# q and k of the first twelve tiles in 2-KB rows on one queue, their bias from 64-row matmuls, and a new order

## Chip, cores and metric

The kernel runs on one core of a Trainium2 chip. The metric is the time of one execution on the device, in microseconds (us). Five engines work side by side, each through its own list of instructions in order: TensorE (PE, with its weight loads as PEld), VectorE (DVE), ScalarE (ACT), GpSimd (POOL) and SyncE (SP), which here issues nearly all DMAs.

## What is computed

Attention with a window of 96 keys, 8 global keys and a linear bias by distance, for 4 batches of 8 heads, 768 positions and 64 columns; its output, as 3072 rows of 512, goes through three products whose maximum is taken, and a last product.

```python
B, H, S, D = q.shape                                    # 4, 8, 768, 64
scores = scale * np.matmul(q, k.transpose(0, 1, 3, 2))
is_global = pos[None, :] < 8
is_local = (rel >= 0) & (rel < 96)
dist = np.where(is_global & ~is_local, 96.0, np.abs(rel))
scores = scores - slopes[:, None, None] * dist
scores = np.where(is_global | is_local, scores, -1e9)
a = softmax(scores)
x = np.matmul(a, v).transpose(0, 2, 1, 3).reshape(B * S, H * D)
h = np.maximum(np.maximum(x @ w1, x @ w2), x @ w3)      # 512 -> 768
out = h @ w_out                                         # 768 -> 512
```

## The kernel before, in words

The 3072 rows are 24 tiles of 128. A batch has six tiles; two neighbouring tiles make a part n (0 to 11), which is what one load of q (s = 0), k (s = 1) or v brings. The tiles are grouped into seven chunks of 4, 2, 2, 4, 4, 4 and 4 tiles for the expert products.

All work is cut into units, and a text, SCHEDULE, lists the units in the order in which their instructions go to the engines. A unit is a letter, its indices and, last, a number that says how it is done (0 for ACT, 1 for DVE, 2 for POOL in most of them). No scheduler moves anything afterwards: each engine runs its own share of the list in order and waits for what it needs.

- `l`, `v`, `w`, `o` load a part of q or k (line 156), a part of v, expert weights (line 478) and output weights. A part of q or k is read either in 512-byte rows (two positions of a head) or in 2-KB rows (eight positions); `short_rows` (line 149) decides: parts 6 to 11, and k of parts 0 to 2, have 512-byte rows. All loads are on SP's queue, but k of part 0, which is on ACT's.
- `c` casts a part of q or k to bf16 (line 179), `C` a half of v (line 190), `W` and `Q` weights. `x` (line 243) transposes a cast part on PE into PSUM and copies it to qkT, or, with 9, by a DMA.
- `Y` and `V` copy pieces of v, `G` (line 229) the global keys, `Z` (line 207) the first tile's keys into a tile of their own, kf.
- `S` (line 293) computes the scores of tile T for half of the heads (g): for each, matmuls of 64 rows (the 64 columns of a head) and 128 columns, two heads at a time in the two halves of the array, then the exponential on ACT (line 317) into P. In the first tiles (last index 1) the bias is added in PSUM ahead of the scores, by two matmuls of the identity with bias (line 299); later tiles multiply P by wmask, the exponential of the bias, on DVE (`M`, line 329). `K` (line 324) makes wmask of a head on ACT, `B` (line 319) the bias.
- `A` (line 338) multiplies P by v and normalises on DVE; `T` (line 376) transposes the result to xT, on PE with a copy (0, 1, 6, 8) or by a DMA (4).
- `F` c.f.j (line 417) is the product of chunk c with the columns f of expert j: four matmuls into one of three PSUM buffers (h), then a cast on ACT for j = 0, a maximum on DVE for j = 1 and 2. `O` (line 451) is the output product of a tile and its store, `E` the last tiles.
- `D` puts matmuls of zeros on PE at the start.

The lines that a sentence cannot say are those of the scores and of the bias:

```python
296         if how:
298             for hh in range(2):
299                 nc.tensor.matmul(sp[:, hh, :, 0:n], identb, bias[:, g, hh, :, sets(T)],
300                                  start=True, stop=False, skip_group_check=True)
301         for ds in range(n):
302             for i in range(2):
303                 jp = 2 * g + i
304                 for z in range(2):
305                     hsl = slice(64 * z, 64 * z + 64)
306                     nc.tensor.matmul(sp[:, z, i, ds], k_cols(T, hsl, jp, ds), q_cols(T, hsl, jp),
```

Of the kernel before, what the change touches and what calls it, by code (L numbers as in the profile page):

```python
# [12 lines left out]
FP32 = mybir.dt.float32  # L13
# [12 lines left out]
    K7 l1.0 c1.0.2 K6 l1.1 B6.1 D0.4 D4.4 B5.1 D2.0 D5.4 K0 c0.1.1 c0.0.1 K2 D8.0 B0.1 B4.0 B1.0  # L26
    B3.0 x0.1.3 K1 K3 K5 c1.1.2 B7.0 x0.0.7 D1.1 D9.2 S1.0.1 Z0.1 B2.1 v0 C0.0.2 S1.1.1 G1.0 x1.0.8
    K4 M1.0 S0.0.1 M0.0 v1 x1.1.8 S2.1.1 S2.0.1 M2.0 C0.1.2 Y0.1.2 Y1.0.1 M1.1 V2.1 Y0.0.1 G2.1 A1.2
    S0.1.1 C1.0.2 C1.1.2 Y2.0.0 Y1.1.2 D3.1 S3.0.1 M3.0 M0.1 A0.2 S3.1.1 M3.1 l2.0 c2.0.2 x2.0.6
    T1.1 M2.1 A2.0 V3.2 T0.0 G3.0 A3.1 l2.1 c2.1.2 x2.1.6 T2.1 w0.0 W0.0.0 l3.0 w0.1 S4.0.1 M4.0  # L30
    T3.8 V4.2 W0.1.2 S4.1.0 D7.1 G4.0 w0.2 F0.1.0 F0.0.0 S5.1.0 c3.0.1 x3.0.6 M4.1 w1.0 W1.0.0
    S5.0.0 F0.1.1 W0.2.2 F0.1.2 v2 C2.0.0 C2.1.0 W2.0.1 F0.0.1 F0.0.2 M5.0 F0.3.0 F0.2.0 M5.1 Y2.1.1
    V5.1 F0.5.0 w1.1 W1.1.0 W2.1.1 F0.4.0 A4.1 A5.0 F0.5.1 T4.0 F0.4.1 w1.2 W1.2.0 l3.1 T5.1 F0.2.1
    F0.2.2 l4.0 c4.0.1 W2.2.0 F0.5.2 c3.1.0 x3.1.7 Z1.0 F0.4.2 F1.0.0 F1.2.0 l4.1 c4.1.1 S7.0.0
    S6.1.0 l5.0 x4.0.6 l5.1 o0 F1.0.1 F1.0.2 c5.0.1 M7.0 F1.3.0 F1.4.0 F1.4.1 o2 c5.1.1 x4.1.7
    S6.0.0 S7.1.0 G7.0 v3 F1.2.1 F1.2.2 F1.3.1 Q2.1 F0.3.1 M7.1 Q0.0 F1.5.0 F1.5.1 S8.0.0 x5.0.7
    S8.1.0 G8.1 C3.0.2 C3.1.1 Y4.0.1 F0.3.2 F1.5.2 A7.0 F1.4.2 F1.1.0 M6.0 x5.1.6 v5 o1 Q1.0 v4
    S9.0.0 S9.1.0 l7.0 l6.1 C5.0.1 C5.1.0 F1.1.1 F1.3.2 Y3.1.1 M8.0 F1.1.2 T7.0 v6 l6.0 M6.1 v7
    Y3.0.1 M9.0 O0.2.1 l7.1 C4.0.0 O0.0.0 G9.0 V8.1 A6.1 c7.0.1 M8.1 c6.1.1 x6.1.9 O0.3.0 C4.1.0
    Y4.1.1 O0.1.1 Y5.1.0 S10.1.0 T6.8 V9.1 M9.1 S10.0.0 O1.0.0 A8.1 M10.1 T8.4 F2.0.0 x7.0.9 G10.0  # L40
    F2.4.0 c6.0.0 l8.1 v9 l9.1 F2.0.1 F2.1.0 M10.0 F2.0.2 S11.0.0 c7.1.0 Y5.0.1 x6.0.6 S11.1.0 V10.1
    F2.1.1 M11.0 F2.4.1 C6.0.0 A9.0 F2.2.0 V11.1 l9.0 O1.1.1 S13.1.0 x7.1.6 S13.0.0 G13.0 M11.1
    F2.2.1 F2.1.2 C6.1.1 F2.2.2 A11.1 F2.3.0 F2.5.0 A10.0 Y6.1.0 Z2.0 F2.4.2 T11.0 F2.5.1 F2.3.1
    C7.0.0 S12.1.0 T9.8 S12.0.0 F2.3.2 v8 C7.1.1 F2.5.2 M12.0 S14.1.0 T10.6 S14.0.0 c8.1.0 O2.0.0
    l8.0 M13.0 G14.1 Y7.1.1 M12.1 F3.2.0 V15.0 M13.1 c9.1.1 x9.1.9 F3.0.0 Y7.0.1 A13.1 F3.3.0 l11.1
    T13.4 M14.0 x8.1.9 M14.1 F3.0.1 S15.1.0 Y6.0.0 S15.0.0 F3.3.1 F3.3.2 F3.1.0 M15.0 M15.1 V14.0
    F3.4.0 c8.0.1 c9.0.0 x9.0.9 l10.0 F3.0.2 A12.1 F3.2.1 x8.0.9 C9.0.0 C8.0.0 A14.0 F3.1.1 T12.4
    l10.1 G15.1 Y8.0.1 c11.1.0 O2.1.0 A15.1 F3.5.0 F3.1.2 C9.1.1 F3.2.2 T15.8 S19.0.0 M19.0 S19.1.0
    c10.0.0 T14.4 C8.1.0 Y8.1.0 F3.4.1 l11.0 v10 F3.5.1 F3.5.2 F3.4.2 Y10.0.1 M19.1 Z3.1 S16.0.0
    S16.1.0 G16.1 V20.0 O3.3.0 O3.2.1 A19.1 F4.5.0 c10.1.1 x10.1.9 v11 F4.1.0 V16.1 G19.1 x10.0.9  # L50
    Y9.0.1 S18.1.0 S17.0.0 M17.0 M16.1 F4.3.0 F4.3.1 F4.5.1 M16.0 V17.1 F4.1.1 S17.1.0 S18.0.0
    F4.2.0 Y9.1.0 O3.0.0 M18.0 M17.1 C10.0.1 M18.1 A16.1 F4.1.2 T19.4 O3.1.1 A18.0 A17.1 C11.0.1
    c11.0.0 x11.0.9 F4.0.0 F4.2.1 F4.2.2 F4.3.2 T18.4 S20.1.0 S20.0.0 T16.4 T17.4 x11.1.9 C10.1.1
    Y10.1.1 F4.0.1 G20.1 F4.0.2 F4.5.2 S21.0.0 S21.1.0 G21.0 M20.0 F4.4.0 F4.4.1 C11.1.1 F4.4.2
    M21.1 F5.1.0 F5.2.0 V21.1 O4.2.1 F5.3.0 Y11.1.0 F5.3.1 M20.1 S22.0.0 S22.1.0 F5.2.1 F5.5.0
    Y11.0.0 F5.2.2 V23.1 F5.4.0 A20.1 F5.3.2 M22.0 M21.0 G22.0 S23.0.0 M23.0 S23.1.0 T20.4 F5.5.1
    O4.1.1 A21.1 T21.4 M23.1 M22.1 O4.0.0 V22.0 F5.4.1 F5.0.0 A23.1 T23.4 O4.3.0 A22.0 F5.4.2 F5.5.2
    F5.0.1 F5.1.1 F5.0.2 T22.4 F5.1.2 F6.3.0 F6.5.0 F6.4.0 F6.5.1 F6.4.1 F6.4.2 O5.1.0 F6.3.1 F6.1.0
    O5.3.1 F6.1.1 F6.0.0 F6.0.1 F6.0.2 O5.0.1 F6.2.0 F6.2.1 F6.3.2 O5.2.0 F6.2.2 F6.1.2 F6.5.2 E
    D6.0  # L60
"""


@with_exitstack
def kernel(
# [13 lines left out]
    nc = tc.nc  # L79
# [13 lines left out]
    sizes = [4, 2, 2, 4, 4, 4, 4]  # L93
# [36 lines left out]
    bias = persist.tile([128, 2, 2, 2, 3, 128], BF16, name="bias")  # L130
    vo_first = [persist.tile([128, 2 * H * 65], BF16, name=f"vof{i}") for i in range(2)]
    vo_next = [persist.tile([128, 2 * H * 65], BF16, name=f"vo{i}") for i in range(2)]
    ve = [persist.tile([128, 2 * H * 65], BF16, name=f"ve{i}") for i in range(2)]
    vf = [persist.tile([128, H * 65], BF16, name=f"vf{i}") for i in range(2)]
# [440 lines left out]
```

## Time and profile before

| what | value |
| --- | --- |
| time, median of 3 runs | 176.9 us (176.84 to 177.01) |
| profiled execution: its span, first to last instruction | 174.9 us |
| median less that span | 2.0 us |
| first expert matmul (h) starts | 21.8 us |
| last matmul ends | 171.5 us |
| PE busy | 169.3 us, 97% |
| DVE, ACT, POOL busy | 132.5, 120.1, 14.3 us |
| read from and written to memory | 25.17 and 6.29 MB |

The profile is of one execution, whose time is told by its span; the runs' times also hold what lies around the span, here 2.0 us. In the rows of the timeline the columns are the start, the length in us (of a group, from its first start to its last end), the engine, the line, the operation, the tiles written and read, their shapes and the count; in brackets stands the idle time ahead of it and what ended it. In a row of the chain they are start, length, engine, tile and line. In a row of groups, the total, the mean of one in ns, and the idle time ahead.

### The profile page before, as it was taken

To read this page: it belongs to the slowest core of one execution; us is meant where nothing else is said; L and a number is where in the kernel's file an instruction comes from. 1 tells how busy PE (TensorE), PEld (TensorE's weight loads), DVE (VectorE), ACT (ScalarE), POOL (GpSimd) and SP (SyncE) were. 2 spreads that over 40 slices of the span, in tenths; PEclk is the share of its full clock that TensorE was granted. 3 is DMA by queue.
4 is the path that set the end of the run, shared out by engine and by line. 5 is a ranking of instruction groups with operands and counts; after the bars stand their busy time and mean duration, and the time that the engine had idled before them with its cause. 6 is when DMAs were issued, how large, how long until landed. Compare 5 with 4: busy or idle time off the path is not lost.

```text
span 174.9 us, 4233 instructions
## 1 busy us (share of the span) xinstructions
PE 169.3 (97%) x1683; PEld 93.0 (53%) x1683; DVE 132.5 (76%) x288; ACT 120.1 (69%) x188; POOL 14.3 (8%) x25
## 2 busy tenths in 40 slices
PE   6999999999999999999999999999999999999992
PEld 2445654658684587754545545544455544444451
DVE  6668859889999999998978769995569873444510
ACT  6989999789988999999948977345594413121132
POOL 5269250000100000000000000000000000000000
PEclk9999999999999999999999999999999999999999
DMA  4999999999999999976999997563101750031205
GB/s 137 347 302 335 359 350 383 385 380 312 309 282 265 298 289 228 292 213 193 257 195 185 304 233 172 166 133 60 54 10 30 105 171 0 0 119 36 89 27 213
DMA packets 55507, 35.92 MB, mean 205 GB/s; under 512 B 18368, under 2 KB 47936, under 8 KB 55488
## 3 DMA queue, kind: packets, MB, share of 16 engines
q1 hardware_dynamic: 54304, 35.07, 73.9%
q10 hardware_dynamic: 1184, 0.59, 1.3%
q8 instruction: 13, 0.21, 0.5%
q14 instruction: 6, 0.05, 0.1%
HBM read 25.17 MB, written 6.29 MB: 180 GB/s over the span
## 4 chain that ended last, share of the span: by engine, by line
PE 94%; ACT 2%; DVE 1%; issue 1%; ACTq 0%; DVEq 0%
PE h L424 53%; PE po L439 18%; PE sp L306 7%; PE op L360 6%; PE wp L504 4%; PE tpr L261 2%; PE sp L299 2%; PE xtp L411 1%; ACT qkT L268 1%; ACT wo L496 1%; PE oph L360 1%; ACT P L317 1%; PE xtr L401 0%; PE tpp L282 0%; DVE qkT L285 0%
## 5 line engine op out<-in xcount | busy, mean ns | idle before, releaser
L424 PE MATMUL h<-xT,w 128*128 128x512 bf16 (+1 forms) x504 | 100.8, 349 | 0.0
L424 PEld LDWEIGHTS <-w 128*128 128x128 bf16 x504 | 46.7, 98 | 40.7 <-ACT w L493 0.6
L317 ACT ACTIVATE P<-sp 128x1024 bf16<-128x1024 f32 (+1 forms) x48 | 44.0, 956 | 9.2 <-PE sp L306 9.1
L429 ACT CAST h<-h 128x512 bf16<-128x512 f32 (+1 forms) x42 | 21.9, 531 | 22.1 <-PE h L424 22.1
L439 PE MATMUL po<-wo,ht 128*128 128x512 bf16 (+2 forms) x156 | 34.1, 363 | 0.0
L431 DVE TENSOR_TENSOR h<-h,h 128x512 bf16<-128x512 bf16 (+1 forms) x42 | 25.2, 605 | 10.9 <-PE h L424 8.9
L433 DVE TENSOR_TENSOR ht<-h,h 128x512 bf16<-128x512 bf16 (+1 forms) x42 | 25.5, 609 | 6.3 <-PE h L424 5.0
L334 DVE TENSOR_TENSOR P<-P,wmask 128x1024 bf16<-128x1024 bf16 x33 | 22.0, 684 | 2.0 <-ACT P L317 1.9
L439 PEld LDWEIGHTS <-ht 128*128 128x128 bf16 x156 | 14.3, 98 | 15.1 <-DVE ht L433 0.2
L448 ACT COPY ost<-po 128x512 f32<-128x512 f32 (+2 forms) x16 | 8.8, 553 | 15.8 <-PE po L439 15.3
L373 DVE TENSOR_TENSOR xb<-op,rz 128x512 bf16<-128x512 f32 x22 | 15.2, 692 | 0.8
L360 PEld LDWEIGHTS <-P 128*128 128x128 bf16 x352 | 13.4, 97 | 4.4 <-issue 0.7
L306 PE MATMUL sp<-qkT 64*128 64x128 bf16 x320 | 14.3, 218 | 0.1
L306 PEld LDWEIGHTS <-qkT 64*128 64x128 bf16 x320 | 9.3, 94 | 8.2 <-issue 5.1
L448 DVE COPY ost<-po 128x512 f32<-128x512 f32 (+1 forms) x10 | 6.5, 647 | 8.4 <-PE po L439 8.4
L188 DVE CAST qkp<-rawp 128x1024 bf16<-128x1024 f32 x12 | 8.2, 687 | 1.7 <-DMA rawp<-in_k_dram 1.6
L504 PE MATMUL wp<-zeros 128*128 128x512 bf16 x17 | 7.1, 559 | 1.5 <-DVE zeros L518 1.4
L188 ACT CAST qkp<-rawp 128x1024 bf16<-128x1024 f32 x8 | 8.4, 1050 | 0.0
L268 ACT COPY qkT<-tpr 128x512 bf16<-128x512 bf16 x12 | 6.6, 588 | 1.0 <-PE tpr L261 1.0
L268 DVE COPY qkT<-tpr 128x512 bf16<-128x512 bf16 x6 | 4.0, 688 | 3.9 <-PE tpr L261 3.9
L372 DVE RECIPROCAL rz<-op 128x8 f32<-128x8 f32 x22 | 4.4, 199 | 2.5 <-PE op L360 2.3
L360 PE MATMUL op<-vo,P 128*128 128x65 bf16 x128 | 5.4, 193 | 0.3 <-issue 0.3
(84 smaller groups left out, 127.9 us busy)
## 6 DMA issues: line engine op xcount, KB each, us to landing
rawv<-in_v_dram SPq DMA_DIRECT2D x12, 512.0 KB, 7.0
out_dram<-ost SPq DMA_DIRECT2D x23, 256.0 KB, 2.4
rawp<-in_k_dram SPq DMA_DIRECT2D x8, 512.0 KB, 5.9
rawp<-in_q_dram SPq DMA_DIRECT2D x12, 256.0 KB, 5.8
wst<-in_moe_w_dram SPq DMA_DIRECT2D x3, 1024.0 KB, 11.5
rawp<-in_q_dram SPq DMA_DIRECT2D x6, 512.0 KB, 6.2
wst<-in_moe_w_dram SPq DMA_DIRECT2D x3, 512.0 KB, 8.5
rawp<-in_k_dram SPq DMA_DIRECT2D x6, 256.0 KB, 8.6
```

What stands on the lines that cost most here:

```text
L188: copies[how](qk, src)
L306: nc.tensor.matmul(sp[:, z, i, ds], k_cols(T, hsl, jp, ds), q_cols(T, hsl, jp), start=not how, stop=True, skip_group_check=True)
L317: nc.scalar.activation(dst, src, AF.Exp, bias=0.0, scale=scale)
L334: nc.vector.tensor_mul(P, P, wmask[:, g, :, 0:2])
L360: nc.tensor.matmul(o, P[:, i, ds], vs[ds][:, h], start=(ds == 0), stop=(ds == len(vs) - 1), skip_group_check=True)
L373: nc.vector.tensor_tensor(out=x.rearrange("p (g h) d -> p g h d", g=2), in0=o4[:, :, :, 0:64], in1=rz[:, :, :, None].to_broadcast([128, 2, ...
L424: nc.tensor.matmul(ps, w123[f // 2][:, dm, j, (f % 2) * 128:(f % 2) * 128 + 128], xT[c][:, dm], start=(dm == order[0]), stop=(dm == order[ ...
L429: nc.scalar.copy(h01, ps)
L431: nc.vector.tensor_max(h01s[c, f], h01s[c, f], ps)
L433: nc.vector.tensor_max(ht[c][:, f], h01s[c, f], ps)
L439: nc.tensor.matmul(po, ht[c][:, f, tt * 128:(tt + 1) * 128], wo[:, f, cols], start=(f == 0), stop=(f == NF - 1))
L448: copy(ost, po)
```

## The change

- Parts 0 to 5 of q and k are all read in 2-KB rows: `SHORT` is empty, so k of parts 0 to 2 changes. All of them are on SP's queue. For k this also changes the pattern of the copy after the transposes (the one of 2-KB rows in place of that of 512-byte rows).
- The bias of the first tiles is built by matmuls of 64 rows. Their weights are the identity scaled by a head's slope (`slope_id`, made by `B`, 192 columns so that both halves can be cut from it), their moving side the distances in bf16 (`rbqb`, and `rbqs` with its halves of rows exchanged). For each half of the heads there are eight such matmuls of 256 columns in place of two of 128 rows and 512 columns. To fit this, the pairs of heads are dealt to g in another way (`jp = 2 * i + g`).
- kf and the unit `Z` are gone: a batch's first tile takes its keys from qkT by matmuls of 64 rows and 64 columns, eight in place of four.
- The tiles of v are views of one tile, vall, whose columns of ones one memset fills instead of eight.
- The identity is made first on POOL, the distances behind it.
- `U` is `S` for both halves. The tiles with a biased half 0 were 0 to 4 and 0 to 3 for half 1; now tiles 0 to 3 have both.
- New ways: casts split between two engines (`c` with 3 to 5), copies of v by a DMA (`Y` with 3).
- SCHEDULE is another list. By its units, x of 20 tiles is transposed by a DMA (`T` with 4) where 12 were; POOL takes 14 casts of q and k for 4, 12 of v for 5, 4 of weights for 2, and 21 copies of v's pieces for 4; the matmuls of zeros are 14 for 17.

The core of the diff, with the list itself left out:

```diff
     def short_rows(n, s):
-        return n >= 6 or (s == 1 and n < 3)
+        return n >= 6 or (n, s) in SHORT
...
-            dma = nc.scalar if (n, s) == (0, 1) else nc.sync
-            dma.dma_start(out=r, in_=src.rearrange("h (i e) d -> i h (e d)", e=2))
+            queues[how].dma_start(out=r, in_=src.rearrange("h (i e) d -> i h (e d)", e=2))
...
-                nc.sync.dma_start(out=r[:, z], in_=src[4 * z:4 * z + 4].rearrange("h (i e) d -> i h (e d)", e=ET))
+                queues[(how + z * (how == 2)) % 2].dma_start(out=r[:, z], in_=src[4 * z:4 * z + 4].rearrange("h (i e) d -> i h (e d)", e=ET))
...
         if how:
-            for hh in range(2):
-                nc.tensor.matmul(sp[:, hh, :, 0:n], identb, bias[:, g, hh, :, sets(T)],
-                                 start=True, stop=False, skip_group_check=True)
+            for i in range(2):
+                for part in range(2):
+                    for z in range(2):
+                        rows = slice(64 * z, 64 * z + 64)
+                        nc.tensor.matmul(sp[:, z, i, 0:n], slope_id[rows, 4 * z + 2 * i + g, 64 * part:64 * part + 128],
+                                         (rbqb, rbqs)[part][rows, sets(T)],
+                                         start=(i == 0 and part == 0), stop=False, skip_group_check=True)
         for ds in range(n):
             for i in range(2):
-                jp = 2 * g + i
+                jp = 2 * i + g
                 for z in range(2):
                     hsl = slice(64 * z, 64 * z + 64)
+                    if T % NT == 0:
+                        for e in range(2):
+                            nc.tensor.matmul(sp[64 * e:64 * e + 64, z, i, 0], qkT[T // NT][hsl, 1, e, jp, 0:64],
+                                             q_cols(T, hsl, jp), start=not how, stop=True, skip_group_check=True)
+                        continue
...
     def u_B(h, how):
-        mul(bias[:, g, z, i], rbq, -slopes[h] / scale)
+        mul(slope_id[:, h], ident, -slopes[h] / scale)
...
-    K7 l1.0 c1.0.2 K6 l1.1 B6.1 D0.4 D4.4 B5.1 D2.0 D5.4 K0 c0.1.1 c0.0.1 K2 D8.0 B0.1 B4.0 B1.0
+    B7.0 l0.0.0 D0.4 D5.6 K2 B2.1 B3.1 c0.0.3 l0.1.0 c0.1.1 x0.0.6 B0.2 B4.2 B6.0 B1.0 D6.2 B5.1
```

What the list changes is seen on the engines. ACT's rows from its start to the first cast of an expert product (h), before. Here wmask is the exponential of the bias, P that of the scores, tpr and xtp are transposes in PSUM, wst a raw weight:

```order
L326 ACTIVATE wmask<-rbq 128x384 x4
L322 ACTIVATE bias<-rbq 128x384 x3
L326 ACTIVATE wmask<-rbq 128x384 x3
L322 ACTIVATE bias<-rbq 128x384
L268 COPY qkT<-tpr 128x8x64 x2
L317 ACTIVATE P<-sp 128x1024 x2
L233 COPY qkT<-qkT 128x8x4
L326 ACTIVATE wmask<-rbq 128x384
L317 ACTIVATE P<-sp 128x4x128
L317 ACTIVATE P<-sp 128x1024 x2
```

ACT's rows now, from the first P to the last wmask (slope_id is the scaled identity; the three wmask and three slope_id ahead of the first P are not shown):

```order
L333 ACTIVATE P<-sp 128x1024 x4
L241 COPY qkT<-qkT 128x8x4
L276 COPY qkT<-tpr 128x8x64 x2
L333 ACTIVATE P<-sp 128x1024
L431 COPY xT<-xtp 128x4x128
L333 ACTIVATE P<-sp 128x1024 x2
L448 CAST h_680<-h 128x512
L333 ACTIVATE P<-sp 128x1024
L276 COPY qkT<-tpr 128x8x64
L448 CAST h_718<-h 128x512
L345 ACTIVATE wmask<-rbqb 128x384 x2
L333 ACTIVATE P<-sp 128x1024 x2
```

Five of the eight wmask rows have moved from ACT's start to behind the first casts of h (three more follow the last row shown), and the weight cast that stood ahead of the first h is no longer on ACT. Ahead of the four P shown first stand two P, a cast of v, two P of a first tile and half a cast of q.

DVE's rows in the first chunk's expert products, from the first maximum, before (P<-P,wmask is a mask, h<-h,h and ht<-h,h are the maxima of an expert product):

```order
L334 TENSOR_TENSOR P<-P,wmask 128x1024
L431 TENSOR_TENSOR h_605<-h_605,h 128x512
L433 TENSOR_TENSOR ht<-h_605,h 128x512
L493 CAST w_2_119<-wst 128x4x256
L431 TENSOR_TENSOR h_612<-h_612,h 128x512
L433 TENSOR_TENSOR ht<-h_612,h 128x512
L334 TENSOR_TENSOR P<-P,wmask 128x1024 x2
```

The same place now:

```order
L450 TENSOR_TENSOR h_718<-h_718,h 128x512
L450 TENSOR_TENSOR h_680<-h_680,h 128x512
L512 CAST w_2_112<-wst 128x4x256
L452 TENSOR_TENSOR ht<-h_718,h 128x512
L452 TENSOR_TENSOR ht<-h_680,h 128x512
L353 TENSOR_TENSOR P<-P,wmask 128x1024 x2
L512 CAST w_1_111<-wst 128x4x256
L353 TENSOR_TENSOR P<-P,wmask 128x1024 x4
L450 TENSOR_TENSOR h_817<-h_817,h 128x512
```

Six masks and a weight cast now stand in one run ahead of the next maximum; before, masks stood between maxima in ones and twos. POOL, which before had two weight casts left at this time and then almost nothing, now runs this:

```order
L199 CAST qkp<-rawp 128x1024
L512 CAST w_0_110<-wst 128x4x256
L208 COPY vall<-vall 64x520
L208 COPY vall<-vall 4x520
L512 CAST w_1_111<-wst 128x4x256
L202 CAST vall<-rawv 128x8x64
L208 COPY vall<-vall 64x520
L208 COPY vall<-vall 4x520
L512 CAST w_1_111<-wst 128x4x256
L199 CAST qkp<-rawp 128x1024
```

These are weight casts, casts of q and v, and copies of v's pieces that ACT and DVE did before.

More of the change, by code (lines that the diff above doesn't have):

```diff
@@ L187, in cast_part @@
         qb["p", n, s] = qk
+        if how >= 3:
+            for z, copy in zip(range(2), split[how - 3]):
+                if short_rows(n, s):
+                    copy(qk[:, z], src[:, z])
+                else:
+                    copy(qk[:, :, z], src[:, :, z])
+            return
         copies[how](qk, src)
@@ L518 @@
         nc.vector.memset(zeros, 0.0)
-        near, own = rbq[:, 0:2].rearrange("p s (e i) -> p s e i", e=2), rbq[:, 2]
+        make_identity(nc, identb)
+        nc.vector.tensor_copy(ident[:, 128:192], ident[:, 0:64])
+        nc.gpsimd.iota(dist, base=128, pattern=[[-1, 2], [1, 2], [2, 64]], channel_multiplier=-2,
+                       allow_small_or_imprecise_dtypes=True)
+        near, own = rbqb[:, 0:2].rearrange("p s (e i) -> p s e i", e=2), rbqb[:, 2]
         nc.gpsimd.affine_select(out=near, in_=dist, compare_op=ALU.is_ge, fill=BIGD, base=128,
@@ L523 @@
                                 pattern=[[1, 2], [-1, 2], [-2, 64]], channel_multiplier=2)
[L524 removed]
+        nc.gpsimd.memset(rbqb[0:NG // 2, 0:2], float(NL))
+        gap = rtmp[:, 0]
+        nc.vector.tensor_scalar(out=gap, in0=dist[:, 0].rearrange("p e i -> p (e i)"), scalar1=shift, scalar2=None, op0=ALU.add)
         nc.vector.memset(far, BIGD)
```

134 lines of the change are left out of this document (65 added, 69 removed).

## The prediction

> **What bounds the kernel now.** I read the page first, then the busy time by stretches, then the chain and the timelines of the start. TensorE (PE) is busy for 97% of the span and makes 94% of the chain that ends last.
>
> ```profile
> span 174.9 us, 4233 instructions
> ...
> PE 169.3 (97%) x1683; PEld 93.0 (53%) x1683; DVE 132.5 (76%) x288; ACT 120.1 (69%) x188; POOL 14.3 (8%) x25
> ...
> PE 94%; ACT 2%; DVE 1%; issue 1%; ACTq 0%; DVEq 0%
> ```
>
> A busy PE may still be a waiting PE, so I split the span where the first expert matmul (h) starts, at 21.8 us, and ask for busy time and for PE's waits in each part.
>
> ```profile
> 8.30:21.80 13.50, 12.84 (x234) 7.53 (x234) 10.81 (x29) 12.33 (x20) 8.53 (x12) 1.00 1.14 330
> 21.80:171.50 149.70, 149.64 (x1412) 82.53 (x1411) 116.53 (x236) 100.86 (x156) 3.02 (x3) 1.00 0.73 193
> ```
>
> The columns after the length are PE, weight loads, VectorE (DVE), ScalarE (ACT), GpSimd (POOL), the granted clock, the DMA share and GB/s. From 21.8 us on PE is busy for 149.64 of 149.70 us, at full clock, and the list of its waits is empty for that stretch. The groups of the chain there have the length of their columns:
>
> ```profile
> 24.48 7.01 PE h L424 x32
> ...
> 34.42 0.22 PE xtp L411 x4
> ...
> 72.95 0.11 PE sp L306 x4
> ...
> 91.85 0.22 PE xtr L401 x8
> ```
>
> 32 h matmuls in 7.01 us are 0.876 us for each product of four, waiting included. So the stage after 21.8 us is bound by PE's own work, and only work taken off PE, or new waits, can change it. Ahead of 21.8 us it is another engine:
>
> ```profile
> 3.11 2.10 ACT L326 ACTIVATE wmask<-rbq 128x384 bf16<-128x384 f32 x4 [0.43 <-DVE rbq L530]
> 5.12 1.33 ACT L322 ACTIVATE bias<-rbq 128x384 bf16<-128x384 f32 x3
> ...
> 8.27 1.04 ACT L268 COPY qkT<-tpr 128x512 bf16<-128x512 bf16 x2
> 9.80 1.94 ACT L317 ACTIVATE P<-sp 128x1024 bf16<-128x1024 f32 x2 [0.49 <-PE sp L306]
> 11.62 0.22 ACT L233 COPY qkT<-qkT 128x32 bf16<-128x32 bf16 x1
> ...
> 12.24 0.60 ACT L317 ACTIVATE P<-sp 128x512 bf16<-128x512 f32 x1
> ...
> 18.86 0.58 ACT L412 COPY xT<-xtp 128x512 bf16<-128x512 bf16 x1
> ...
> 20.54 1.05 ACT L493 CAST w<-wst 128x1024 bf16<-128x1024 f32 x1
> ...
> 23.41 1.09 ACT L429 CAST h<-h 128x512 bf16<-128x512 f32 x2
> ```
>
> From the first exponential (P) at 9.80 to the cast of the first weights, which ends at 21.59, ACT hardly rests (12.33 of the 13.5 us above). The first h follows that cast. After the last matmul, from 171.5 to 174.9, come a copy and a store, 3.4 us, which the change does not touch.
>
> **The first expert matmul.** To cost it I need the rows of DVE and PE at the start too:
>
> ```profile
> 7.45 0.41 PE L261 MATMUL tpr<-identb,qkp 64*128 64x64 bf16 x16
> ...
> 10.90 1.29 DVE L268 COPY qkT<-tpr 128x512 bf16<-128x512 bf16 x2 [1.61 <-PE tpr L261]
> ...
> 14.74 0.16 DVE L364 RECIPROCAL rz<-oph 128x4 f32<-128x4 f32 x1
> ...
> 14.94 0.42 DVE L365 TENSOR_TENSOR xb<-oph,rz 128x256 bf16<-128x256 f32 x1
> ...
> 18.40 0.20 DVE L372 RECIPROCAL rz<-op 128x8 f32<-128x8 f32 x1
> 18.63 0.69 DVE L373 TENSOR_TENSOR xb<-op,rz 128x512 bf16<-128x512 f32 x1
> ...
> 20.91 0.41 DVE L412 COPY xT<-xtp 128x512 bf16<-128x512 bf16 x1
> 21.27 0.49 DVE L404 COPY xT<-xtr 128x256 bf16<-128x256 bf16 x2
> ```
>
> Step one is when the first P can start. The landings are read from the engines that waited for them:
>
> ```profile
> 5.56 0.69 DVE L188 CAST qkp<-rawp 128x1024 bf16<-128x1024 f32 x1 [1.59 <-DMA rawp<-in_k_dram]
> ...
> 6.41 0.69 DVE L188 CAST qkp<-rawp 128x1024 bf16<-128x1024 f32 x1 [0.16 <-DMA rawp<-in_q_dram]
> ...
> 7.40:11.40 4.00, 3.84 (x63) 1.98 (x62) 2.19 (x4) 3.51 (x7) 2.11 (x3) 1.00 1.21 292
> 30.00:38.00 8.00, 8.00 (x86) 4.40 (x85) 7.29 (x15) 6.23 (x9) 0.00 (x0) 1.00 1.05 384
> ```
>
> The stretch from 7.4 to 11.4 us carries rows of 512 bytes, at 292 GB/s; the one from 30 to 38 carries rows of 2 KB, at 384 GB/s. A load of 524 KB takes 1.80 us at the one rate and 1.37 at the other, so each of the three k loads that change their rows saves 0.43 us. Before, k and q of tiles 0 and 1 are there at 6.41; with both in 2-KB rows I put it at 6.0. One queue instead of two may cost start-up: from nothing up to 1 us. From there, by rows: cast 0.69, sixteen transposes 0.41, two DVE copies of 0.65 (the long rows need the pattern of line 268, in place of a faster one), scores 0.4 and 0.1 of handing over; that is 8.9 us for the first P, 0.9 earlier than now.
>
> Step two is ACT's list from there to the copy of tile 2's transposed x, in the new order (the second piece of order above, and what the sentence behind it names): two P 1.94, a v cast and half a q cast of 0.6 each (as the half P), two half P 1.2, four P 3.9, a small copy 0.22, two transposed copies 1.04, one P 0.97, the copy 0.58. These are 11.1 us, and about 0.5 for two places where the list waits for its own last result (the scores of tile 2 behind DVE's copies, those of tile 4 behind ACT's). That gives 20.5. DVE has its own list. After the first scores it copies the transposed k and q of the second load, 2 x 1.29, done at 12.4. Then, to the copy that ends tile 3: three pairs of half normalisations (4 x 0.58 + 1.2 = 3.5), half a cast and a v cast 0.8, two copies 1.29, two small ones 0.4, one normalisation 0.89, and xT copies of 0.41, 0.49 and 0.41: 8.2 to 8.5 us, so 20.9. The first weights are the tenth load, 6.0 + 5 x 1.37 + 3 x 1.80 = 18.3 at the latest; POOL's cast of them (1.2, shown below) ends by 19.5 and does not gate. So **the first h starts at 20.9** instead of 21.81. Of the seven wmask exponentials and four bias scalings that ACT does ahead of the first P now (0.53 and 0.44 each), three and three remain, the latter on half the columns.
>
> The bias matmuls cost the same if the 64-row ones run in pairs: eight of 256 columns in pairs are four times 107 ns, as two of 512 columns are now. The row that bears on it is the scores' own, eight 64-row matmuls of 128 columns in pairs; the group of four above takes 0.11 us, half of what four in sequence need at 53 ns. Bounds: nothing to 0.43 us more per unit, eight units. They lie beside P (0.97 each), so I take nothing.
>
> **After the first h.** Before, 149.7 us of PE work follow. Eight transposes of x go from PE to the DMA queue (tiles 4, 5, 6, 7, 9, 10, 11, 15), at the 0.22 of the rows above: 1.8 us less. Scores of tile 5 (0.22) and x of the fourth k load (0.23) now stand ahead of the first h: 0.45 less. The first tiles of three batches use eight matmuls of 64 rows by 64 columns in place of four: between 0.11 us (four at a time) and 0.22 (pairs) per unit, six units, 0 to 0.7 more; I take 0.3. That leaves 147.8 us.
>
> The Trainium skill's page "TensorEngine Tiling (Array Packing)", Key Properties, says that different tiles of the array can run weight loads and matmuls in parallel, and lists four tiles for 64x64. The trace agrees for two (0.11 us for four); no run here shows four. By the page my 0.3 would be 0, and the last matmul at 169.4.
>
> ```profile
> xT<-xb SPq DMA_TRANSPOSE x12, 2.5
> ...
> 38.40:80.00 41.60, 41.55 (x573) 28.74 (x573) 40.00 (x95) 39.13 (x68) 0.62 (x1) 1.00 1.05 276
> ```
>
> Then comes a new wait. Five wmask exponentials now stand between ACT's h casts. By the rows ACT runs from 20.5: two P, an h cast (0.55) to 23.0; P, copy, h cast to 25.0; two exponentials, two P, three exponentials to 29.6; then the casts of the h of columns 4, 5, 2, 3 are done at 30.1, 30.9, 32.5 (a weight cast of 1.05 stands between) and 33.0. PE reaches the tenth product after nine (7.9), scores and transposes (1.1), at 29.9; h has three PSUM buffers, so this one needs column 4's, free at 30.1, and the twelfth, at 31.9, needs column 2's, free at 32.5. That is 0.2 + 0.6, and I add 0.2 for the DMA transpose of tile 5, which lands about when the next chunk begins (2.5 us to land). **1.0 us**, with bounds of 0 and 4.
>
> Weights: w2's first piece is the twelfth load instead of the eleventh, 1.37 later, less 3 times 0.43: it lands when it does now. The copies that go from ACT and DVE to POOL, the k copies for first tiles that vanish, the one memset in place of eight: none is on PE's path after 21.8 us. DVE is busy for 40.0 of the 41.6 us from 38.4 to 80, ACT for 39.1, and still PE waits for neither; both get less to do. I cost them at nothing, and the first rival says what it is if that cover goes.
>
> The sum, in the profiled execution: 20.9 + 147.8 + 1.0 = 169.7 us for the last matmul, where it is 171.5 now. That is 1.8 us less: a span of 173.1 instead of 174.9. The median of the runs, 176.9, lies 2.0 above the span; with that unchanged, **175.1 us**.
>
> **The rivals.**
>
> *DVE and POOL block each other: slower.* POOL goes from 14 us of work to about 40.
>
> ```profile
> 13.21 1.59 POOL L191 CAST vo<-rawv 128x512 bf16<-128x512 f32 x2 [0.20 <-DMA rawv<-in_v_dram]
> ...
> 14.23 0.59 DVE L233 COPY qkT<-qkT 128x32 bf16<-128x32 bf16 x1
> ...
> 21.68 0.68 DVE L188 CAST qkp<-rawp 128x1024 bf16<-128x1024 f32 x1
> 21.89 2.53 POOL L493 CAST w<-wst 128x1024 bf16<-128x1024 f32 x2 [3.20 <-DMA wst<-in_moe_w_dram]
> L233 DVE COPY qkT<-qkT x7: 155/171/594, 14.2 to 117.3; 128x32 bf16<-128x32 bf16 x7
> L493 POOL CAST w<-wst x2: 1040/1200/1359, 21.9 to 23.4; 128x1024 bf16<-128x1024 f32 x2
> L334 DVE TENSOR_TENSOR P<-P,wmask 128x1024 bf16<-128x1024 bf16 x33 | 22.0, 684 | 2.0 <-ACT P L317 1.9
> ```
>
> A DVE copy whose median is 171 ns took 594 and ended with POOL's cast, at 14.8; a POOL cast that began under a DVE cast took 1359 ns, the next one 1040. So each holds the other off. In the new order DVE has seven operations in a row, six masks of 0.68 and a weight cast, before the maxima that free h's buffers; POOL has some 5 us of copies and casts for the same time. One by one, they would put DVE back by up to 4.5 us, and PE with it, three buffers later. Taken at 3.8: 178.9. It decides from 1.8 us on. Against it: DVE's copies out of PSUM beside POOL were not longer, and half of DVE's work after 21.8 us reads PSUM. The Trainium skill's page "SBUF — State Buffer", Who interferes with whom, speaks against this change: a DVE instruction with two SBUF inputs contends with a GpSimd one that reads SBUF, and the second fully blocks. The two rows agree for copies and casts; no row shows it for the masks. By that rule 178.9 is nearer than the forecast.
>
> *The list on ACT is shorter than I think: faster still.* If the first loads land a whole us earlier on the one queue, ACT's list starts at 8.0, and the exponentials fall into holes: 20.0 + 147.5 + 0 = 167.5, 4.0 less, 172.9. For it: ACT was full from 9.8 on, so every us there counts. Against: v's landing also holds the list.
>
> *The 64-row bias does not run in pairs: no change.* Then a unit is 0.86 + 0.22 on PE, over P's 0.97; with the changes of tile shape 0.2 to 0.3 more per unit, about 0.9 in all to the first h, and a stall of 2 instead of 1: 21.8 + 147.8 + 2 = 171.6, or 177.0.
>
> **How the numbers follow.** Forecast 0.42, its own range 173.6 to 176.5; faster still 0.20; blocking 0.24; no change 0.14. About 0.2% is what a measurement of this kernel can tell from none, 176.55 to 177.25. Faster takes the first two and a little of the last: 0.63; within 0.2%: 0.11; slower 0.26. The range leaves out a fifth, a part of the fastest case (0.08) and half of the slowest (0.12): 172.4 to 178.9.
>
> **What would show it.** In the new profile: first P near 8.9, first h near 20.9, the last matmul near 169.7; PE waits of some 1 us between 29 and 34 us for ACT's h casts, and none after; DVE's masks between 27 and 34 us at 0.68 each (beyond 0.9 the blocking is right); the first tiles' score group of eight at 0.11 to 0.22 us. I am wrong if the first h starts after 21.8, if the list of PE's waits after 40 us is not empty, or if DVE's maxima rather than ACT's casts hold the buffers.

## The result and the profile after

The changed kernel takes **188.45 us** (median of 4 runs, 187.2 to 189.64), the kernel before 176.87 beside it: a ratio of 1.066, 95% interval 1.061 to 1.070. The forecast of 175.1 is 13 us too low, and the range ended at 178.9. All times below are medians; the kernel before stood at 176.76 to 176.88 beside each of the runs. Some executions of a kernel come out over 1.5% above its fastest, and these are left out of the medians of the experiments.

The page of the changed kernel (busy times, the DMA share by slices of 4.7 us, the DMA queue, the chain that ends last):

```profile
span 186.6 us, 4323 instructions
...
PE 167.9 (90%) x1689; PEld 93.9 (50%) x1710; DVE 128.9 (69%) x263; ACT 102.9 (55%) x165; POOL 45.1 (24%) x64
...
DMA  5899999938999999789998899877202333101116
...
q1 hardware_dynamic: 57520, 36.78, 75.6%
...
PE 49%; DMA 28%; DVE 7%; SPq 5%; ACT 3%; POOL 3%; issue 2%; ACTq 0%; POOLq 0%; DVEq 0%
PE h L443 31%; DMA rawv<-in_v_dram 12%; PE po L458 12%; DMA rawp<-in_k_dram 10%; DMA qkT<-qkp 5%; PE op L379 3%; SPq L171 3%; PE sp L322 2%; DVE h L450 2%; DMA xT<-xb 2%; DVE P L353 2%; ACT P L333 1%; SPq L167 1%; POOL qkp L199 1%; DVE xb L392 1%
```

The chain was 94% PE before. Now 28% of it are DMAs: loads of v and k, and transposes. The other engines are *less* busy than before, all but POOL. From the first expert matmul to 0.2 us before the last matmul ends, at 183.4 (the stretch for which the prediction had 148.8 us):

```profile
23.10:183.20 160.10, 149.40 (x1343) 81.99 (x1364) 111.92 (x214) 85.97 (x138) 30.59 (x38) 0.99 0.75 185
```

PE is busy for 149.40 of 160.10 us, so it stands for 10.7 us, where it stood for 0.06 before. The list of PE's waits (total, times, longest) names 9.3 of them; the rest are gaps of 0.05 to 0.3 us, in part where a matmul's record is missing. Its rows, the largest first:

```profile
PE h L443 <- ACT h L448: 3.1, 1, 3.1
...
PE sp L322 <- DMA qkT<-qkp: 1.5, 2, 1.3
PE h L443 <- DMA xT<-xb: 1.5, 2, 1.2
...
PE oph L379 <- DVE h L450: 1.3, 1, 1.3
```

The chain shows what stands behind them (start, length, what):

```profile
41.60 3.04 DMA rawp<-in_k_dram
...
45.43 8.62 DMA rawv<-in_v_dram
...
79.18 7.12 DMA rawv<-in_v_dram
...
86.90 0.59 ACT h L448
...
87.53 0.59 PE h L443
...
104.66 7.26 DMA rawp<-in_k_dram
...
113.11 4.35 DMA qkT<-qkp
...
126.70 3.48 DMA xT<-xb
```

One of them followed through: v of part 8 is issued at 79.18 and lands at 86.30, since other transfers stand ahead of it. ACT's list has its cast ahead of an h cast; the h cast at 86.90 gives back the buffer for which PE waits 3.1 us, until 87.53. The row of PE's wait names ACT; the cause is a load.

The queue's own time is its share of the span. Before it was

```profile
q1 hardware_dynamic: 54304, 35.07, 73.9%
```

or 129.3 us of 174.9 on 16 engines; now it is 75.6% of 186.6, or 141.1. The packets of the queue took 12 us more, most of it in those of 256 bytes: the eight added transposes bring 4096 more of them, and all of them together took 34.3 us, 23.9 before.

### The profile page after: what moved, and what is told of

Its sections match the earlier page's. It is cut to its first block, busy times and chain, and to the rows that moved or that the text cites. A ratio compares the mean times of both kernels' runs of the same rounds, so it can differ in the third digit from the quotient of the medians.

```text
span 186.6 us, 4323 instructions
## 1 busy us (share of the span) xinstructions
PE 167.9 (90%) x1689; PEld 93.9 (50%) x1710; DVE 128.9 (69%) x263; ACT 102.9 (55%) x165; POOL 45.1 (24%) x64
## 3 DMA queue, kind: packets, MB, share of 16 engines
q1 hardware_dynamic: 57520, 36.78, 75.6%
## 4 chain that ended last, share of the span: by engine, by line
PE 49%; DMA 28%; DVE 7%; SPq 5%; ACT 3%; POOL 3%; issue 2%; ACTq 0%; POOLq 0%; DVEq 0%
PE h L443 31%; DMA rawv<-in_v_dram 12%; PE po L458 12%; DMA rawp<-in_k_dram 10%; DMA qkT<-qkp 5%; PE op L379 3%; SPq L171 3%; PE sp L322 2%; DVE h L450 2%; DMA xT<-xb 2%; DVE P L353 2%; ACT P L333 1%; SPq L167 1%; POOL qkp L199 1%; DVE xb L392 1%
## 5 line engine op out<-in xcount | busy, mean ns | idle before, releaser
L353 DVE TENSOR_TENSOR P<-P,wmask 128x1024 bf16<-128x1024 bf16 x34 | 25.4, 760 | 6.1 <-ACT P L333 6.0
L199 POOL CAST qkp<-rawp 128x1024 bf16<-128x1024 f32 x14 | 14.5, 1038 | 41.3 <-DMA rawp<-in_k_dram 25.1
L208 POOL COPY vall<-vall 4x520 int32<-4x520 int32 (+2 forms) x21 | 13.3, 635 | 37.6 <-DVE vall L208 18.5
L322 PE MATMUL sp<-qkT 64*128 64x128 bf16 x320 | 13.5, 217 | 3.4 <-DMA qkT<-qkp 1.5
L392 DVE TENSOR_TENSOR xb<-op,rz 128x512 bf16<-128x512 f32 x18 | 12.4, 691 | 0.6
L202 POOL CAST vall<-rawv 128x512 bf16<-128x512 f32 x12 | 9.5, 798 | 13.6 <-DMA rawv<-in_v_dram 13.6
L379 PE MATMUL op<-vall,P 128*128 128x65 bf16 x264 | 10.4, 193 | 0.1
L276 DVE COPY qkT<-tpr 128x512 bf16<-128x512 bf16 x11 | 7.3, 684 | 1.2 <-PE tpr L269 1.2
L202 ACT CAST vall<-rawv 128x512 bf16<-128x512 f32 x7 | 4.3, 635 | 6.4 <-DMA rawv<-in_v_dram 6.4
```

The lines of the kernel that those rows point to most:

```text
L199: copies[how](qk, src)
L353: nc.vector.tensor_mul(P, P, wmask[:, g, :, 0:2])
L379: nc.tensor.matmul(o, P[:, i, ds], vs[ds][:, h], start=(ds == 0), stop=(ds == len(vs) - 1), skip_group_check=True)
L392: nc.vector.tensor_tensor(out=x.rearrange("p (g h) d -> p g h d", g=2), in0=o4[:, :, :, 0:64], in1=rz[:, :, :, None].to_broadcast([128, 2, ...
```

## The experiments

The theories, as they came up: **A**, the added DMA transposes; **C**, rows and queue of the first loads; **S** and **L**, stores or late loads in SP's one in-order queue; **P**, POOL's work; **D**, the time of the DMA queue as a whole; **O** (B in the first runs), the order of the engines' work. "Old list" is the list of the kernel before.

### Which part of the change costs

**Eight transposes back on PE**, at their places in the new list (e1), and the reverse in the kernel before (e4):

```diff
-T4.4 ... T5.4 ... T6.4 ... T7.4 ... T9.4 ... T10.4 ... T11.4 ... T15.4
+T4.0 ... T5.1 ... T6.8 ... T7.0 ... T9.8 ... T10.6 ... T11.0 ... T15.8
```

> The changed kernel with the eight transposes of x (tiles 4, 5, 6, 7, 9, 10, 11, 15) back on TensorE, at the same places of the list. Theory A, the DMA queue: the eight added DMA transposes (1.2 us of SyncE's queue each, and the queue stands still behind each until its tile is normalised) make the loads of v and k late, and TensorE starves; then about 180 us, 8 less than 188.4, with the idle DMA slice near 40 us filled. Theory B, the order: the new list asks for its loads and its casts on GpSimd too late whatever carries the transposes; then 186 to 189 us, TensorE's 1.8 us of added work included.

Measured: **190.44** (ratio 1.077, 1.071 to 1.083). Not better but 2.0 worse, about the PE work that came back. A alone is out. The queue's time is down again to what it was before the change, 68.2% of 189.5 us, or 129.2, so the 12 us added to the queue are not by themselves the loss.

> The kernel before with the same eight transposes of x moved from TensorE to the DMA queue, at their old places in the list. Theory A: 182 to 186 us, since the loads behind them on the queue become late. Theory B: 175 to 178 us, 1.8 us of TensorE's work less, and a wait of 1 or 2 us where a transpose stands close ahead of its first user.

Measured: **195.38** (1.107, 1.103 to 1.111). In the old list the same eight transposes cost 18.6 us, more than either theory had (the granted clock was 0.96 there, so a part may be the clock). In its chain the PE waits for them:

```profile
69.84 3.69 DMA xT<-xb
...
88.59 4.35 DMA xT<-xb
```

So a transpose by DMA is cheap or dear by the list it stands in.

**The old list in the changed code**, with the old rows and queues (e2), and with the new rows on one queue (e3):

```diff
-SHORT = []
+SHORT = [(0, 1), (1, 1), (2, 1)]
+        load_part(0, 1, 1)
+        load_part(0, 0)
```

> The changed kernel's code with the old list (without the unit for the first tiles' own key copy, one bias unit earlier), the old rows and the old two queues: what is left of the change is the bias by 64-row matmuls, the first tiles' keys from the common tile, and one tile for v. Theories A and B: 176 to 177.5 us, the same as before within 0.5. Theory D, the 64-row bias matmuls are dear (not in pairs): 1 to 3 us more, and the first expert matmul later than 22.8 us.

> As the kernel with the old list, but with all of q and k of the first six parts in 2-KB rows and all on SyncE's queue. Theory C, rows and queue: in the changed kernel's start the loads came at some 280 GB/s instead of 384 and the fourth landed at 10.9 us instead of 9.5; if the 2-KB rows on one queue do that, this costs 1 to 2 us against the kernel with the old list, first expert matmul 1 to 2 us later. If the slow start belongs to the new list, it is within 0.3 us of it.

Measured: **177.09** (1.0014, 1.0005 to 1.0024) and **178.48** (1.009, 1.007 to 1.011). The 64-row bias, the missing copies of k and the one memset cost 0.3 us together. Rows and queue cost 1.4 in the old list, as C has it. All else, 10.0 us, comes with the new list.

**The old start in the new list** (e6: the edit of e2, the list without its first two loads):

> The changed kernel with the old start of the loads: k of parts 0 to 2 in 512-byte rows, k of part 0 on ACT's queue and q of part 0 on SP's, both ahead of everything; the rest of the list as changed. Theory C (rows and one queue cost 1.6 us, as measured on the old list, and add to the rest): 186.5 to 187.5. Rival (in the new list the start is given back by later waits for loads): 188 to 189, no change.

Measured: **188.09** (1.064, 1.063 to 1.066). That is the rival's time, but not its mechanism: the first h starts at 23.7 us, against 23.1 in the changed kernel, so the old rows and queues gain nothing at the start of the new list that later waits could give back.

**Each half of the list by itself**: old up to the first h of chunk 2, then new (e10), and the reverse (e11).

> The changed code with the old list and the old start of the loads up to the first matmul group of chunk 2, and from there the new list. Whichever half holds the loss keeps it: if the loss of the new list sits ahead of chunk 2 (by the lag of the matmul groups 3.7 us of it do), 180 to 184 here; if the second half brings 7 us or more by itself, 184 to 188.

> The other way round: the new list up to the first matmul group of chunk 2, then the old list, with the old start of the loads. If the second half of the new list holds the larger loss, 179 to 182; if the first half does (late loads carry into the second half whatever its order), 184 to 188.

Measured: **183.81** (1.042, 1.035 to 1.048) and **184.57** (1.045, 1.041 to 1.049). Against e2's 177.1 each half brings about 7 us; there is no one bad place, and the two do not add up, since the whole new list brings 11.4.

### Is it the place of loads and stores in SP's queue?

SP stands long at the stores, in the new kernel:

```profile
SPq L468 <- DVE ost L467: 22.7, 5, 8.9
SPq L468 <- ACT ost L467: 21.1, 7, 7.7
```

So the stores went to ACT's queue (e5):

```diff
-    def f2_out(po, c, tt, copy, cols=slice(0, DM), dma=nc.sync):
+    def f2_out(po, c, tt, copy, cols=slice(0, DM), dma=nc.scalar):
```

> The changed kernel with one edit: the stores of the output are issued by ACT and no longer by SP; list, loads and transposes stay. Theory S (SP works its DMAs off in order; in the changed kernel SP stood 22.7 + 21.1 us at the line of the stores, waiting for the copies into ost, and the loads of v and k behind those stores went out late): loads go out earlier, 179 to 185 us. Theory X (the loads go out late for the casts that give their buffers back and for the DMA engines' own time, the stores stand beside that): within 1.5 us of the changed kernel, 187 to 190. ACT's own issue of 28 stores may cost up to 1 us under either.

Measured: **189.29** (1.070, 1.065 to 1.076). S falls. SP stands at the next thing instead, a transpose whose x isn't there yet:

```profile
SPq L400 <- DVE xb L392: 27.9, 3, 14.7
```

**Loads earlier**, 25 of them (e7), all three at once (e8), and only the eight latest (e9):

```diff
-T8.4 F2.4.1 U13.0 ... A11.1 T11.4 F2.3.0 C6.0.1 l8.1 ... l9.0 ... l9.1 ... v9
+T8.4 F2.4.1 v9 l9.1 l8.1 U13.0 ... A11.1 l9.0 T11.4 F2.3.0 C6.0.1 ...
```

(The piece is e9's, and `v9` is v of part 9, `l8.1` k of part 8.)

> The changed kernel with 25 loads of q, k and v (parts 3 to 11) moved up in the list to just behind the cast that frees their buffer, none ahead of the last load of the first weights; everything else in place. Theory L (the new list asks for its loads too late, the DMA engines stand idle at 38 to 40 us and at 78 to 80 us, and POOL's casts, the transposes and the PE wait for the data): 178 to 184. Rival X (the DMA engines are what limits, by bytes and by transposes, or the buffers come free late): 187 to 190. A third way: SP blocks at a load whose buffer is still in use and holds stores and transposes back: above 190.

> The changed kernel with three edits at once: the 25 loads moved up, the stores issued by ACT, and the eight transposes of the attention output back on the PE. If SP's one in-order queue is where the new list loses (theories S and L), this is the least loaded SP of all and comes to 177 to 181 (the PE does 1.8 us more work). If the loss lies in the order of the computing itself (casts, exponentials and maxima on POOL, DVE and ACT), it stays at 186 to 191.

> The changed kernel with eight loads of parts 8 to 11 (k8, q9, k9, v9, q8, q10, k10, k11), which the new list asks for 4 to 23 us of PE work later than the old list does, put back to the place that they have in the old list by PE work; the loads of parts 0 to 7, the stores and the transposes stay. Theory L2 (only these late loads are too late; moving all 25 loads blocked the DMA queue ahead of the transposes of the first tiles): 182 to 185, the 3.7 us stand ahead of chunk 3's second group gone. Rival X (the DMA engines' time is the limit, earlier loads delay transposes and stores by as much): 187 to 192.

Measured: **204.24** (1.156, 1.154 to 1.158), **201.99** (one run, so no interval) and **201.94** (1.139, 1.135 to 1.143). Asking earlier for data made it 13 to 16 us slower: L and L2 fall, and rival X, which had at most 192, had the direction and not the size. e7's time is that of its third way; for e9 the half loads below show that a buffer still in use is not the mechanism, for e7 no run shows it. In e9, SP's issues, and then the chain:

```profile
76.23 0.53 SPq L178 DMA_DIRECT2D rawv<-in_v_dram  x1
76.81 2.29 SPq L167 DMA_DIRECT2D rawp<-in_k_dram  x2
79.20 1.66 SPq L468 DMA_DIRECT2D out_dram<-ost  x1
80.96 1.26 SPq L400 DMA_TRANSPOSE xT<-xb  x1
82.27 0.57 SPq L167 DMA_DIRECT2D rawp<-in_q_dram  x1
82.94 3.47 SPq L400 DMA_TRANSPOSE xT<-xb  x1
```

```profile
82.94 6.47 DMA xT<-xb
...
89.54 0.58 PE h L443
```

The transpose that chunk 3 needs is issued at 82.94, behind v, two k, a store, another transpose and q; it lands after all of them, 6.47 us later, and PE's h waits. What is moved ahead in the queue puts back what stands behind.

**The loads on ACT's queue**, to part the one order of SP from the time of the DMA engines (e17):

```diff
-l4.0 ... l11.1
+l4.0.1 ... l11.1.1
-        nc.sync.dma_start(out=r, in_=v[b, ...
+        (nc.sync, nc.scalar)[n > 2].dma_start(out=r, in_=v[b, ...
```

> The changed kernel with the loads of q and k of parts 4 to 11 and of v of parts 3 to 11 issued by ACT, on its queue; transposes, weights and stores stay with SP, the list stays. Theory F (what costs is the one order of SP's queue: loads held at SP behind stores and transposes, transposes behind the loads' bytes): 180 to 185. Theory D (the DMA engines' time for the bytes and transposes is the limit, whichever queue brings them): 186 to 191. ACT standing at a load whose buffer is still in use would cost on top: above 191.

Measured: **199.98** (1.131, 1.129 to 1.133). In the third band: a load on ACT keeps ACT's own place in the list, and POOL then waits for q and k.

```profile
POOL qkp L199 <- DMA rawp<-in_q_dram: 22.7, 3, 13.3
...
POOL qkp L199 <- DMA rawp<-in_k_dram: 20.2, 5, 9.1
```

It does not part the two.

### Is it the DMA queue's time?

**Half the bytes of q, k and v**, in the new list (e13), in the old list as its control (e14), and in e9's list (e16):

```diff
-            queues[how].dma_start(out=r, in_=src.rearrange("h (i e) d -> i h (e d)", e=2))
+            queues[how].dma_start(out=r, in_=src[0:4].rearrange("h (i e) d -> i h (e d)", e=2))
...
-            for z in range(2):
+            for z in range(1):
...
-in_=v[b, :, k * 256:k * 256 + 256, :]
+in_=v[b, 0:4, k * 256:k * 256 + 256, :]
```

> The changed kernel with its list untouched, but q, k and v are loaded for heads 0 to 3 alone, and each cast reads those for heads 4 to 7 too: half the bytes of these loads (9.4 of 18.9 MB left out), rows as long as before, the engines' work as before; the output is not the reference's for heads 4 to 7. Theory D (in the new list the compute units stand so that they need data just when the DMA queue, busy with loads, stores and transposes one behind the other, has it not yet; the DMA queue's time is what the PE waits for): 170 to 178. Rival O (the order of the casts, exponentials and maxima is at fault, loads only show in the waits): 184 to 189.

> The control for the half loads: the changed code with the old list and the old start, the same half of q, k and v loaded (output not the reference's for heads 4 to 7). The old list measured 177.1 with full loads and its chain of waits is 97% PE work, so both theories expect 173 to 177: what the start gains, and little else.

> The list of the run with eight late loads put back (201.9) and half the bytes of q, k and v (output not the reference's for heads 4 to 7). Theory D (the earlier loads cost because transposes and stores stood behind their bytes in the one queue): within 2 us of the half loads in the changed list. Rival B (SP stood at a load whose buffer was still in use, bytes or not): 10 us or more above the half loads in the changed list.

Measured: **181.08** (1.022, 1.018 to 1.025), **177.14** (1.002, 1.001 to 1.003) and **181.39** (1.025, 1.023 to 1.027). e13 lies between the bands of D and O, so neither has it whole. Its difference from the changed kernel tells the most: with the same work on the compute engines and the same list, half the bytes give back 7.4 us in the new list, nothing in the old one (177.09 with all bytes; both theories had at most 177), and 20.5 in e9's list, as D has it there; with half the bytes the eight loads cost the same in either place. Half the bytes also take 12 of SP's 36 issues of q and k away, about 0.6 us each, and no run parts the two. The pages of e13 and of e14:

```profile
span 180.1 us, 4307 instructions
...
q1 hardware_dynamic: 43504, 27.34, 57.1%
...
PE 66%; DVE 14%; DMA 8%; ACT 5%; issue 4%; SPq 1%; DVEq 0%; ACTq 0%
```

```profile
span 175.8 us, 4366 instructions
...
q1 hardware_dynamic: 39696, 25.89, 52.1%
...
PE 89%; DVE 8%; issue 1%; ACT 0%; ACTq 0%
```

The DMA part of the chain goes from 28% to 8%. Where the time comes back shows in the start of each chunk's first h (its first weight load, us):

| | chunk 0 | 1 | 2 | 3 | 4 | 5 | 6 | last matmul ends |
|---|---|---|---|---|---|---|---|---|
| changed | 23.1 | 43.3 | 55.1 | 79.2 | 103.6 | 130.3 | 157.1 | 183.4 |
| e13, half the bytes | 21.4 | 40.9 | 51.8 | 76.5 | 97.4 | 123.6 | 150.4 | 176.7 |
| e9, late loads back | 24.1 | 44.6 | 56.8 | 89.5 | 117.9 | 145.1 | 171.9 | 198.2 |
| e16, e9 with half | 20.9 | 40.6 | 51.7 | 77.0 | 97.4 | 123.2 | 150.0 | 176.3 |

Of the 6.7 us at the end, 1.7 come ahead of the first h, 1.6 more by chunk 2, and 3.5 between the starts of the chunks 3 and 4, where v of part 8 was late; by chunk 3 it is 0.6 less, and from chunk 4 on the rows differ by 6.2 to 6.7.

### Is it the engines?

**The old engines in the new order** (e12: casts, moves of v, copies and the eight transposes where the old list has them), and **no DMA transposes at all up to tile 19** (e15):

```diff
-C2.0.2 ... V5.2 ... W1.2.2 ... c4.0.2 ... T4.4
+C2.0.0 ... V5.1 ... W1.2.0 ... c4.0.1 ... T4.0
```

```diff
-x6.1.9 ... T8.4
+x6.1.8 ... T8.8
```

> The changed kernel's order with the old list's engines: POOL's casts and moves of q, k, v and w (45.1 us of POOL's time, against 14.3 before) go back to ACT and DVE where the old list has them, and the eight transposes back to the PE. Theory P (POOL's slow chain gives buffers back late, and blocks DVE): 178 to 183. Theory O (the places in the list are at fault, whatever engine works there): 186 to 192.

> The changed kernel with all DMA transposes of q, k and of the attention output of tiles 0 to 19 put on the PE, at their places in the list (PE +4 us, DVE +10 us of copies). Theory T (transposes and loads in one queue hold each other up: a load behind a transpose landed 2.7 us after it, a load behind a load 1.4): 182 to 188 in spite of the added work. Rival (the loads' places in SP's order are at fault, as with eight transposes on the PE at 190.4): 191 to 200.

Measured: **220.22** (1.246, 1.241 to 1.251) and **205.53** (1.161, 1.155 to 1.167). Both lie above all their bands. P falls: with POOL's work and the eight transposes taken back it is 32 us slower. The likely reason, not shown, is that order and engine were planned together, each unit standing where *its* engine is free. e15 is 17.1 us slower for 6.7 us more PE work (174.6 by its page, 167.9 above) and 11.2 us more of DVE's, so without the transposes in the queue it is not faster, but the added work is not parted from that.

**Half the bytes and the eight transposes on PE** (e18):

> The changed kernel with half the bytes of q, k and v (output not the reference's for heads 4 to 7; 181.1 by itself) and the eight transposes of the attention output back on the PE, 1.8 us of PE work. If the 4 us that the half loads leave above the old list's half loads (177.1) are the time of the transposes in the DMA queue: 177 to 180. If they are the engines' order: 182 to 186.

Measured: **185.48** (1.049, 1.044 to 1.054). The transposes in the queue are not the 4 us that half the bytes leave above the old list: 4.4 us worse without them, in the band for the engines' order. The chain of this run has hardly a DMA left:

```profile
PE 74%; DVE 11%; ACT 9%; issue 3%; DMA 2%; DVEq 0%; ACTq 0%
```

## Why the prediction was wrong, step by step

The forecast of the last matmul was 20.9 + 147.8 + 1.0 = 169.7 us; it ended at 183.4. Of the 13.7 us, the first h is 2.2, PE's work 1.8 (149.6 us, the 149.4 above and the last 0.2) and PE's waits 9.7 (10.7 us). The work was right: in e13, with the same list and a clock of 1.00, it is 147.2 us (the clock was 0.99 here).

**The failed step is the waits after the first h.** The prediction gave them 1.0 us, 0.8 for ACT's h casts and 0.2 for one transpose. It looked at no load after the first weights but the next weights, which "lands when it does now"; whether the loads of q, k and v and the transposes would still come in time had no term, and so cost nothing. In their place the chain is 28% DMA, and the 3.1 us of the longest wait go back to the load of v of part 8. The prediction read from PE's empty list of waits that loads were no bound. That list says that the old list had its data in time, not by how much. The row that spoke against it was quoted there: a DMA share of 1.05 from 38.4 to 80 us, 1.21 at the start, so packets were always under way (a share above 1 means that they overlap), and eight transposes, counted as 1.8 us saved on PE, were put into that queue. How little room such a queue has shows in e4 and e9: the same eight transposes cost the old list 18.6 us, and eight loads moved up cost the new list 13.5.

Halving the bytes shows the size: 7.4 of the 11.6 us by which the kernel got slower hang on the bytes of q, k and v (1.7 of them ahead of the first h). The other 4 us do not; by e18's chain they lie with DVE's and ACT's order and with waits of PE for them, but no run took one such wait away, so that stays argued. Why the new list suffers from bytes that the old one bore is shown for single loads and transposes, as the two followed above, and not for the whole.

Point by point:

- *First P at 8.9, with k and q there at 6.0.* It started at 9.67. k of part 0 is the third and fourth DMA on the one queue, and its cast began at 7.08: a little over the upper bound of 1 us that I had for start-up, where I took nothing. Then ACT and POOL stood for v, whose 0.6 us casts lead the chain to the first h:

```profile
7.08 0.69 DVE L199 CAST qkp<-rawp 128x1024 bf16<-128x1024 f32 x1 [1.79 <-DMA rawp<-in_k_dram]
...
9.67 1.94 ACT L333 ACTIVATE P<-sp 128x1024 bf16<-128x1024 f32 x2
...
12.67 0.62 ACT L202 CAST vall<-rawv 128x512 bf16<-128x512 f32 x1 [1.06 <-DMA rawv<-in_v_dram]
```

- *First h at 20.9.* It was 23.09. ACT's list to the copy of tile 2 ended at 22.47 where I had 20.5, DVE's at 22.94 where I had 20.9: both 2.0 later, of which 0.8 by the first P. With half the bytes the first h is at 21.4, so most of the 2.2 us is loads; their old rows and queues do not bring it back (23.7 in e6). The last piece of the chain ahead of it is the blocking of the first rival, a copy with a median of 171 ns that took 0.73 us beside a POOL cast:

```profile
21.55 1.04 POOL L199 CAST qkp<-rawp 128x1024 bf16<-128x1024 f32 x1 [0.42 <-PE xtp L430]
```

```profile
21.89 0.73 DVE L241 COPY qkT<-qkT 128x32 bf16<-128x32 bf16 x1
```

- *The 64-row bias costs nothing, in pairs.* Right: two of 256 columns start every 0.11 us, eight in 0.44, and e2 shows no cost. The rival of 177.0 is out.

```profile
8.73 0.28 PE L309 MATMUL sp<-rbqb,slope_id 64*128 64x256 bf16 x2
8.85 0.27 PE L309 MATMUL sp<-rbqs,slope_id 64*128 64x256 bf16 x2
```

- *0.8 us of waits for ACT's h casts at 29 to 34 us, 0.2 for the transpose of tile 5.* The first did not come: from 28.7 to 36.1 PE's h matmuls run without a gap, and from 23.1 to 43.3 its list names one wait, 0.2 us, with no holder. The second did: at 43.0 PE stands for 0.29 us for that transpose. PE was busy for 19.44 of the 20.2 us up to chunk 1's first h; that the rest is near 1.0 is luck.
- *The first tiles' group of eight at 0.11 to 0.22 us.* Right: sixteen start at 39.94 and the next row at 40.28, so 0.17 for eight.
- *None after 40 us.* Wrong; this is the sign that the text itself named.
- *DVE and POOL block each other.* The mechanism is there, its size in the masks is small. All masks (count, shortest, median and longest in ns), and the two runs of them in the stretch that I had named:

```profile
L353 DVE TENSOR_TENSOR P<-P,wmask x34: 673/684/2092, 30.8 to 149.1; 128x1024 bf16<-128x1024 bf16 x34
```

```profile
30.78 1.43 DVE L353 TENSOR_TENSOR P<-P,wmask 128x1024 bf16<-128x1024 bf16 x2
...
32.73 2.90 DVE L353 TENSOR_TENSOR P<-P,wmask 128x1024 bf16<-128x1024 bf16 x4
```

  Six masks took 0.4 us more than six times 0.684, against 3.8 in the rival; over the kernel four masks were long, 2.6 us in sum, one of 2092 ns at 68.66. The rule of the Trainium skill's page "SBUF — State Buffer", Who interferes with whom, fits: these four are the ones that began when a POOL cast or copy still had 0.46 to 0.56 us to run, and they waited for its end, the one of 2092 ns for that of the next cast too. Five masks that began 0.01 to 0.2 us before a POOL operation kept 0.68 to 0.69, and POOL's then took 0.97 to 1.15 us, where the same cast or copy takes 0.62 alone; the other 25 had no more than 0.1 us of POOL beside them. That a slower time came out is no proof of this rival: e12, with POOL's work back at 15.6 us, is the slowest of all.

## What to carry to other kernels

Before work is moved to the DMA queue, or loads are moved in an order, read the DMA share of the stretch: where it was about 1 here, a transfer put ahead delayed those behind it, transposes and stores too (e4, e9), and PE's list of waits, empty in the kernel before, had not told of it. Halving the bytes with the list untouched, with a control in the old list, is a cheap way to tell how much of a loss is late data. An order and an assignment of engines planned together are hard to judge by exchanging one of them: of what was taken back by itself, neither the transposes nor the stores' queue, the start or the engines made this kernel measurably faster; half of the whole list did, by 4 to 5 us (e10, e11).

## What the runs showed of the hardware

- A transfer behind a DMA transpose can start slowly. After the two transposes that landed at 78.27 and 79.08, k of part 8 was in the queue from 77.89 on and landed at 83.84. The columns end with the clock, the DMA share and GB/s:

```profile
78.60:80.40 1.80, 1.71 (x22) 1.07 (x22) 1.77 (x6) 1.24 (x3) 0.00 (x0) 1.00 0.33 51
81.00:82.00 1.00, 1.00 (x6) 0.43 (x5) 1.00 (x3) 0.59 (x1) 0.00 (x0) 1.00 1.16 349
```

  Up to 130 us, of eight loads next behind a transpose four landed 3.0 to 4.8 us after it, where a 512-KB load behind another took 1.75. Part of this may be the time that any load needs from its issue: these four were issued 1.2 to 2.2 us before the transpose landed, the other four, but one of half the size, over 3 us before.
- SP itself is held by each transpose (ns shortest, median, longest), twice as long as by the 0.6 us of most loads:

```profile
L400 SPq DMA_TRANSPOSE xT<-xb x20: 1188/1248/2236, 38.9 to 153.9; - x20
```

- 2-KB rows on one queue did not bring 384 GB/s at the start. From 5 to 10 us, where v's 512-byte rows are among them, the changed kernel moved less than the one before, 283 GB/s against 332 with a share of 1.14, with its DMA engines not full:

```profile
5.00:10.00 5.00, 3.66 (x65) 1.89 (x65) 2.30 (x5) 2.83 (x7) 0.65 (x1) 1.00 0.88 283
```

- Where PE waited most, the granted clock fell, where the kernel before had 1.00: 0.91 from 80 to 100 us. Over a whole execution it was 0.96 in e4, 0.95 in e9 and 0.94 in e12; in e9 PE was busy for 171.7 us, 167.9 in the changed kernel with the same work.

```profile
80.00:100.00 20.00, 16.60 (x117) 8.01 (x117) 12.67 (x26) 10.87 (x17) 2.27 (x3) 0.91 1.08 241
```
